# Sixty-four bytes: the place of eleven weight blocks in SBUF, in an attention and feed-forward kernel on one core

## The chip, the core and the metric

The kernel runs on one core of a Trainium2 chip. The metric is the device time of one execution in microseconds, taken as the median of several; before the change it is 888.88 us (three runs, 888.55 to 888.99). The profile shown here is one execution taken by the hardware profiler.

## The reference: what is computed

A pooled attention feeds a feed-forward layer. With 8 batches, 8 heads, 576 positions and head size 64:

```python
k_p = k.reshape(B, H, Sp, pool, D).mean(axis=3)      # pool = 8, Sp = 72
v_p = v.reshape(B, H, Sp, pool, D).mean(axis=3)
scores = scale * np.matmul(q, k_p.transpose(0, 1, 3, 2))
attn = softmax(scores)
x = matmul(attn, v_p), put together as (4608, 512)
h = x @ w_in                                          # w_in is 512 x 2048
g = np.maximum(h, 0.0) + np.log1p(np.exp(-np.abs(h))) # softplus
out = g @ w_out                                       # w_out is 2048 x 512
```

Everything is float32. Most of the arithmetic lies in the two products of the feed-forward layer.

## The kernel before

**Tiling.** The 4608 tokens are worked in 18 chunks of 256. The 2048 hidden columns are cut into 16 weight blocks of 128; block f has its part of w_in (512 x 128, stored as 128 x 512) and its part of w_out (128 x 512). To reach float32 accuracy each operand is split into a high and a low part of type fp32r, and each product is made of three: high by high, high by low, low by high.

**First product.** `ffn1_products` (L620) and `pair1` (L668) compute h. Here the weights (the stationary operand, which a LDWEIGHTS puts into the array) are 128 x 128 pieces of w_in out of the tiles `w` and `l`, and what streams past them (the moving operand) is x, 256 tokens wide.

**Second product.** Here it is the other way round: the stationary operand is a 128 x 128 piece of g (tiles `gh`, `gl` for the high and the low part, `so` for sums of quarters of g), and what streams is w_out. In the first four chunks (`ffn2`, L642; `pair2`, L709) a moving operand is 512 columns wide. From the fifth chunk on (`pair2_fast`, L817) the four quarter products of a pair of blocks are made from seven instead of eight products, each 256 columns wide. Three of the seven stream w_out itself; four stream sums of its quarters that `combine` made before, called t here. `t_sums`, `t_middle` and `streamed` say where these lie.

**Where the blocks lie.** Weight blocks 0 to 10 are in one SBUF tile, `w`, and blocks 11 to 15 in another, `l` (`LATE = 5`). In every partition such a tile holds n areas of 4096 bytes with w_out (high part, then low part; `parts(f)[:, 0]`), then a room of a few words, then n areas of 4096 bytes with w_in (`parts(f)[:, 1]`), then the room again. Once the first product has no more use for w_in in `w`, the t go over the same ground: `streamed(f)` is an area of 4096 bytes that is counted from the tile's start without the room.

**What sets addresses.** Tiles stand one behind the other in their pool, and `fill` puts a few unused words between them: `FILL[3]` words ahead of `w`, `FILL[0] - ROOM` behind it. Built, `w` begins at byte 10944 of each partition, which is 192 modulo 256. All 128 x 128 pieces of g that are loaded as weights of the second product (`gh`, `gl`, `so` and their like of the first chunks) begin at multiples of 256. The moving operand x of the first product lies at 192 modulo 256, the pieces of w_in that are its weights at 0, and w_out in `l` at 192. So before the change a streamed operand of either feed-forward product begins, modulo 256, 192 bytes after the weights that are loaded while it streams, which are those of the next matmul.

**Order of the work.** A list scheduler inside the kernel (`Order.run`, with a table of small corrections) fixes the order in which each engine gets its instructions; it knows nothing of addresses. SyncE issues all DMAs.

Of the kernel before, what the change touches and what calls it, by code (L numbers as in the profile page):

```python
# [10 lines left out]
F32R = mybir.dt.float32r  # L11
I32 = mybir.dt.int32
# [92 lines left out]
def pooled_attention_softplus_ffn(  # L105
# [12 lines left out]
    NTOK, DM = out.shape  # L118
    DFF = w_in.shape[1]
    P = 128  # L120
# [18 lines left out]
    wpool = ctx.enter_context(tc.tile_pool(name="wpool", bufs=1))  # L139
# [51 lines left out]

    PART, ROOM, LATE = 2 * DM, 16, 5
    BEGINS = [0, FC - LATE, FC]
    FILL = 256 - ROOM, 32, 16, 64
    groups = [None, None]

    def group(f):
        g = 0 if f < FC - LATE else 1  # L200
        n = BEGINS[g + 1] - BEGINS[g]
        if groups[g] is None:
            groups[g] = wpool.tile([P, 2 * (n * PART + ROOM)], F32R, tag="wl"[g], name="wl"[g])
        return groups[g], f - BEGINS[g], n

    def place(w, f, n):
# [2 lines left out]
    def parts(f):  # L209
        return place(*group(f)).rearrange("p i (a n) -> p i a n", a=2)  # L210

    def streamed(f):
        w, f, n = group(f)
        return w[:, (n + f) * PART:(n + f + 1) * PART]

    fill = lambda pool, n, i: n and pool.tile([P, n], F32, tag=f"fill{i}", name="fill")
    fill(wpool, FILL[3], 3)
    group(0)
    fill(wpool, FILL[0] - ROOM, 0)
    stage = wpool.tile([P, 2 * (LATE * PART + ROOM)], I32, tag="l", name="stage")  # L220
    stage_at = lambda i: stage[:, i * 2 * PART:(i + 1) * 2 * PART].rearrange("p (i n) -> p i n", i=2)
    fill(wpool, FILL[1], 1)
    for tag in ("Xha", "Xhb", "Xla", "Xlb"):
        xpool.tile([P, HP, CT], F32R, tag=tag, name="x")
    fill(xpool, FILL[2], 2)
    wi, wo = {}, {}
# [1328 lines left out]
```

## Time and profile before

| what | value |
|---|---|
| median of the runs | 888.88 us (888.55 to 888.99) |
| the profiled execution's own time | 888.88 us |
| its span, first to last instruction | 887.2 us |
| TensorE matmuls (PE), busy | 873.3 us, 98% of the span, 8280 instructions |
| weight loads (PEld), busy | 830.8 us, 94% |
| VectorE (DVE), busy | 646.4 us, 73% |
| ScalarE (ACT), busy | 416.6 us, 47% |
| granted TensorE clock, mean | 0.997 |

A matmul's duration in the profile is longer than its share of the engine's time, since the next begins while it still drains. How fast TensorE goes is therefore read from the distance between the starts of matmuls that follow each other, which the timeline gives: its rows merge neighbours of one kind, with the start of the first and their count.

### The profile page before, as it was taken

To read this page: it belongs to the slowest core of one execution; us is meant where nothing else is said; L and a number is where in the kernel's file an instruction comes from. 1 tells how busy PE (TensorE), PEld (TensorE's weight loads), DVE (VectorE), ACT (ScalarE), POOL (GpSimd) and SP (SyncE) were. 2 spreads that over 40 slices of the span, in tenths; PEclk is the share of its full clock that TensorE was granted. 3 is DMA by queue.
4 is the path that set the end of the run, shared out by engine and by line. 5 is a ranking of instruction groups with operands and counts; after the bars stand their busy time and mean duration, and the time that the engine had idled before them with its cause. 6 is when DMAs were issued, how large, how long until landed. Compare 5 with 4: busy or idle time off the path is not lost.

```text
span 887.2 us, 20509 instructions
## 1 busy us (share of the span) xinstructions
PE 873.3 (98%) x8280; PEld 830.8 (94%) x8280; DVE 646.4 (73%) x1601; ACT 416.6 (47%) x852; POOL 3.8 (0%) x33
## 2 busy tenths in 40 slices
PE   7999999999999999999999999999999999999997
PEld 4689998899999999999999999999999999999997
DVE  5899999788858788677776566778576565747454
ACT  5954343355353545445444435353545354535432
POOL 1000000000000000000000000000000000000000
PEclk9999999999999999999999999999999999999999
DMA  8966544445887778696877575678656565736472
GB/s 261 321 203 210 170 166 159 163 156 201 288 283 225 234 250 266 207 268 197 279 232 223 190 223 205 191 258 252 215 181 232 183 214 178 251 143 236 170 248 83
DMA packets 107086, 191.12 MB, mean 215 GB/s; under 512 B 46064, under 2 KB 60400, under 8 KB 106992
## 3 DMA queue, kind: packets, MB, share of 16 engines
q1 hardware_dynamic: 106992, 189.82, 65.3%
q8 instruction: 65, 1.06, 0.5%
q14 instruction: 29, 0.24, 0.1%
HBM read 167.25 MB, written 22.54 MB: 214 GB/s over the span
## 4 chain that ended last, share of the span: by engine, by line
PE 95%; DMA 2%; DVE 1%; ACT 1%; issue 0%; SPq 0%; DVEq 0%; ACTq 0%
PE h L668 37%; PE m L817 30%; PE acc L642 8%; PE h L620 7%; PE acc L709 3%; PE avp L587 2%; PE qTp L380 2%; PE ptp L461 2%; PE sc L508 1%; PE avp L594 1%; DMA l<-wi 1%; ACT E L425 1%; DMA kvl<-in_v_dram 1%; PE m L508 0%; PE sc L400 0%; PE ltp L561 0%
## 5 line engine op out<-in xcount | busy, mean ns | idle before, releaser
L668 PE MATMUL h<-x,l 128*128 128x256 f32 x2748 | 338.1, 279 | 1.0 <-DMA l<-wi 1.0
L668 PEld LDWEIGHTS h<-x,l 128*128 128x128 f32 x2748 | 324.0, 188 | 2.6 <-DMA l<-wi 1.4
L676 ACT ACTIVATE g<-h 128x512 f32<-128x512 f32 x120 | 71.8, 598 | 286.0 <-PE h L668 285.9
L817 PE MATMUL m<-w,so 128*128 128x256 f32 x1134 | 148.4, 278 | 0.0
L817 PEld LDWEIGHTS m<-w,so 128*128 128x128 f32 x1134 | 138.3, 188 | 0.1
L727 DVE TENSOR_TENSOR sf<-g 128x128 f32<-128x128 f32 x112 | 32.7, 292 | 136.5 <-ACT g L676 136.4
L741 ACT CAST so<-sf 128x512 fp32r<-128x512 f32 x112 | 69.7, 622 | 63.6 <-DVE sf L730 61.0
L817 PE MATMUL m<-w,gh 128*128 128x256 f32 x476 | 92.0, 282 | 0.0
L746 DVE TENSOR_TENSOR so<-sf,so 128x512 fp32r<-128x512 f32 x112 | 77.3, 690 | 17.9 <-ACT so L741 16.1
L817 PEld LDWEIGHTS m<-w,gh 128*128 128x128 f32 x476 | 72.1, 188 | 0.0
L697 DVE TENSOR_TENSOR gl<-g,gh 128x384 fp32r<-128x384 f32 (+1 forms) x120 | 67.2, 560 | 2.4 <-ACT gh L690 2.4
L817 PE MATMUL m<-w,gl 128*128 128x256 f32 x238 | 66.2, 278 | 0.0
L690 ACT ACTIVATE gh<-h 128x384 fp32r<-128x384 f32 (+1 forms) x120 | 59.3, 494 | 0.0
L625 ACT ACTIVATE g<-h 128x256 fp32r<-128x256 f32 x96 | 32.0, 382 | 55.5 <-PE h L620 33.5
L620 PEld LDWEIGHTS h<-x,w 128*128 128x128 f32 x396 | 48.6, 188 | 2.7 <-ACT g L625 0.6
L620 PE MATMUL h<-x,w 128*128 128x256 f32 x396 | 49.8, 278 | 0.2 <-ACT g L625 0.2
L817 PEld LDWEIGHTS m<-w,gl 128*128 128x128 f32 x238 | 44.9, 189 | 0.0
L838 DVE TENSOR_TENSOR o<-o,m 128x256 f32<-128x256 f32 x98 | 39.7, 418 | 4.0 <-PE m L817 0.9
L642 PE MATMUL acc<-w,g 128*128 128x512 f32 x132 | 41.9, 399 | 0.0
L817 PE MATMUL m<-l,gh 128*128 128x256 f32 x196 | 38.1, 283 | 0.0
L730 DVE TENSOR_TENSOR sf<-g,sf 128x128 f32<-128x128 f32 x112 | 32.7, 292 | 3.9
L431 DVE TENSOR_REDUCE sm<-E 128x8 f32<-128x576 f32 x30 | 21.2, 748 | 18.3 <-ACT E L343 18.3
(210 smaller groups left out, 1261.0 us busy)
## 6 DMA issues: line engine op xcount, KB each, us to landing
l<-wi SPq DMA_DIRECT2D x224, 512.0 KB
out_dram<-o SPq DMA_DIRECT2D x36, 256.0 KB
q<-in_q_dram SPq DMA_DIRECT2D x32, 256.0 KB
kst<-in_k_dram SPq DMA_DIRECT2D x24, 288.0 KB
vst<-in_v_dram SPq DMA_DIRECT2D x24, 256.0 KB
stage<-in_moe_w_in_dram SPq DMA_DIRECT2D x22, 256.0 KB
stage<-in_moe_w_out_dram SPq DMA_DIRECT2D x11, 512.0 KB
wi<-w SPq DMA_DIRECT2D x11, 512.0 KB
```

What stands on the lines that cost most here:

```text
L620: nc.tensor.matmul(out=ps[:, 0:CT], lhsT=row(w, kc), rhs=x[:, kc], start=first and kc == j == 0, stop=last and kc == KC - 1 and j == 2)
L642: nc.tensor.matmul(out=accs[c][t], lhsT=a[:, ts], rhs=w, start=f == 0 and j == 0, stop=f == FC - 1 and j == 2)
L668: nc.tensor.matmul(out=ps[:, k * CT:(k + 1) * CT], lhsT=row(w, kc), rhs=x_[c][i][:, kc], start=first and n == 0, stop=last and n == len(or ...
L676: nc.scalar.activation(out=g, in_=x.rearrange("p (b i) -> p b i", i=P), func=AF.Softplus)
L690: nc.scalar.activation(out=gh, in_=quarters(c, x.rearrange("p (b i) -> p b i", i=P)), func=AF.Softplus)
L697: nc.vector.tensor_tensor(out=gl, in0=quarters(c, g), in1=gh.bitcast(F32), op=ALU.subtract)
L727: tt(out=sf[:, 2], in0=g[:, 0], in1=g[:, 2], op=ALU.add)
L730: tt(out=sf[:, 3], in0=g[:, 3], in1=sf[:, 1], op=ALU.subtract)
L741: nc.scalar.copy(out=so[:, 0], in_=ss[c, u])
L746: nc.vector.tensor_tensor(out=so[:, 1], in0=sf, in1=so[:, 0].bitcast(F32), op=ALU.subtract)
L817: nc.tensor.matmul(out=ms[c][n], lhsT=x, rhs=y, start=u == 0 and j == 0 and n in (1, 6, 5, 4), stop=u == FP - 1 and j == 2 and n in (2, 7, ...
L838: nc.vector.tensor_tensor(out=o, in0=in0, in1=m[n], op=how)
```

## The change

The tile `w` gets a room of 32 words in place of 16, `l` keeps its 16; the filling ahead of `w` shrinks from 64 words to 48, and the filling behind it from 224 words to 208. In bytes of a partition: `w` begins 64 lower, at 10880 in place of 10944, and is 128 longer; everything behind it stands where it stood (16 words less ahead, 32 more inside, 16 less behind). The w_out areas of blocks 0 to 10 and the streamed t in `w` move 64 bytes down with the tile. The w_in areas in `w` do not move, since the room in front of them grew by what the start went down. So the streamed operands out of `w` begin at 128 modulo 256 in place of 192, against weights that begin at 0 as before. Every engine has the same instructions in the same order with the same waits.

```diff
-    PART, ROOM, LATE = 2 * DM, 16, 5
+    PART, ROOMS, LATE = 2 * DM, (32, 16), 5
     BEGINS = [0, FC - LATE, FC]
-    FILL = 256 - ROOM, 32, 16, 64
+    FILL = 208, 32, 16, 48
     groups = [None, None]

     def group(f):
         g = 0 if f < FC - LATE else 1
         n = BEGINS[g + 1] - BEGINS[g]
         if groups[g] is None:
-            groups[g] = wpool.tile([P, 2 * (n * PART + ROOM)], F32R, tag="wl"[g], name="wl"[g])
+            groups[g] = wpool.tile([P, 2 * (n * PART + ROOMS[g])], F32R, tag="wl"[g], name="wl"[g])
         return groups[g], f - BEGINS[g], n
...
     fill(wpool, FILL[3], 3)
     group(0)
-    fill(wpool, FILL[0] - ROOM, 0)
-    stage = wpool.tile([P, 2 * (LATE * PART + ROOM)], I32, tag="l", name="stage")
+    fill(wpool, FILL[0], 0)
+    stage = wpool.tile([P, 2 * (LATE * PART + ROOMS[1])], I32, tag="l", name="stage")
```

## The prediction

> **What bounds the kernel now.** First the page: busy times, the granted clock, and the chain of work that ended last.
>
> ```profile
> PE 873.3 (98%) x8280; PEld 830.8 (94%) x8280; DVE 646.4 (73%) x1601; ACT 416.6 (47%) x852; POOL 3.8 (0%) x33
> PEclk9999999999999999999999999999999999999999
> PE 95%; DMA 2%; DVE 1%; ACT 1%; issue 0%; SPq 0%; DVEq 0%; ACTq 0%
> PE h L668 37%; PE m L817 30%; PE acc L642 8%; PE h L620 7%; PE acc L709 3%; PE avp L587 2%; PE qTp L380 2%; PE ptp L461 2%; PE sc L508 1%; PE avp L594 1%; DMA l<-wi 1%; ACT E L425 1%; DMA kvl<-in_v_dram 1%; PE m L508 0%; PE sc L400 0%; PE ltp L561 0%
> ```
>
> TensorE is the end of 95% of the chain at full clock. No instruction moves, so the only way in which the change can reach the time is the distance from one matmul's start to the next. Second, the groups of TensorE instructions with their shapes kept apart: these are the matmuls whose moving operand comes out of `w`, and beside them the largest group, which streams x.
>
> ```profile
> line engine op names shapes xcount | busy us, mean ns | idle before us <-releasers
> L668 PE MATMUL h<-x,l 128*128 128x256 f32 x2748 | 338.1, 279 | 1.0 <-DMA l<-wi 1.0
> L817 PE MATMUL m<-w,so 128*128 128x256 f32 x1134 | 148.4, 278 | 0.0
> L817 PE MATMUL m<-w,gh 128*128 128x256 f32 x476 | 92.0, 282 | 0.0
> L817 PE MATMUL m<-w,gl 128*128 128x256 f32 x238 | 66.2, 278 | 0.0
> L642 PE MATMUL acc<-w,g 128*128 128x512 f32 x132 | 41.9, 399 | 0.0
> L642 PE MATMUL acc<-w,gl 128*128 128x512 f32 x66 | 26.2, 397 | 0.3 <-DVE gl L631 0.3
> L709 PE MATMUL acc<-w,gh 128*128 128x512 f32 x44 | 14.1, 402 | 0.0
> L709 PE MATMUL acc<-w,gl 128*128 128x512 f32 x22 | 8.7, 395 | 0.0
> ```
>
> So 1134 + 476 + 238 = 1848 matmuls of 256 columns and 132 + 66 + 44 + 22 = 264 of 512 columns are touched. Idle time before them is 0.3 us, so there is nothing to win from waits.
>
> Third, the timeline of TensorE at two places with the same kinds of instructions, us from the span's start, the row's length, and its count behind the x. The first is at 435 us:
>
> ```profile
> 435.68 1.58 PE L817 MATMUL m<-w,so 128*128 128x256 f32 x12
> 437.09 0.40 PE L817 MATMUL m<-w,gh 128*128 128x256 f32 x2
> 437.32 0.28 PE L817 MATMUL m<-w,gl 128*128 128x256 f32 x1
> 437.44 2.99 PE L668 MATMUL h<-x,l 128*128 128x256 f32 x24
> 440.27 0.40 PE L817 MATMUL m<-w,gh 128*128 128x256 f32 x2
> ```
>
> The second lies between 592 and 605 us:
>
> ```profile
> 592.57 1.52 PE L817 MATMUL m<-w,so 128*128 128x256 f32 x12
> 593.93 0.39 PE L817 MATMUL m<-w,gh 128*128 128x256 f32 x2
> ...
> 598.68 0.40 PE L817 MATMUL m<-w,gh 128*128 128x256 f32 x2
> 598.92 0.28 PE L817 MATMUL m<-w,gl 128*128 128x256 f32 x1
> ...
> 601.08 2.88 PE L668 MATMUL h<-x,l 128*128 128x256 f32 x24
> 603.80 1.04 PE L380 MATMUL qTp<-ident,q 128*128 128x128 f32 x8
> ```
>
> At 435 us, 12 matmuls that stream `w` take 437.09 - 435.68 = 1.41 us, 117.5 ns each, and 24 that stream x take 2.83 us, 117.9 ns each. At 592 us the 12 take 1.36 us, 113.3 ns each, and at 601 us the 24 take 2.72 us, 113.3 ns each. TensorE thus has **two cadences**, 4.5 ns apart, for the same instructions with the same addresses modulo 256, and both products share them. A cadence holds over long stretches, from one interruption by transposes or scores to the next. Other engines do not tell the two apart; busy times over most of such a stretch, the slow one first:
>
> ```profile
> 423.20:447.90 24.70, 24.70 (x212) 24.70 (x211) 20.70 (x60) 11.77 (x19) 0.00 (x0) 1.00 0.83 266
> 562.80:588.00 25.20, 25.20 (x225) 25.20 (x224) 19.32 (x56) 11.73 (x19) 0.00 (x0) 1.00 0.78 244
> ```
>
> In the columns PE, PEld, DVE, ACT and POOL busy, granted clock, DMA share and GB/s, 212 matmuls in 24.70 us stand against 225 in 25.20, at the same clock, with ACT alike and DVE at 84% against 77%. The slow cadence looks like a relation between the two reads of SBUF that TensorE makes at once, the moving operand and the next weights, that once begun repeats itself. By the distances of the starts in the trace, 579 of the 1848 touched matmuls go at the slow cadence (116 to 125 ns) and 1246 at the fast one (115 or less); among the untouched, 686 of the 2880 of L668 and 129 of the 503 of L817 that stream `l` are slow, and 2135 and 356 are fast.
>
> **The change part by part.** *What is removed or added:* no instruction, wait or transfer. The DMAs into `w` write the same bytes from the same sources 64 bytes lower, and VectorE and ScalarE write and read `w` there during conversion; they get no new work, and TensorE covers them (95% of the chain). Cost nothing; if they were slower, the 1.0 us that L668 waits for DMA in the group above shows how thin their share is.
>
> *What moves:* the moving operand begins 128 instead of 192 bytes after the next weights, modulo 256. No matmul before the change streams from `w` at 128, so the price has to be bounded. The nearest row at 128 is another instruction, a transpose (L380), whose moving operand, the identity, lies at byte 1152, that is 128 modulo 256. The weight loads (PEld) of such a group beside those of x:
>
> ```profile
> 600.97 2.79 PEld L668 LDWEIGHTS h<-x,l 128*128 128x128 f32 x24
> 603.71 0.89 PEld L380 LDWEIGHTS qTp<-ident,q 128*128 128x128 f32 x8
> 604.57 0.30 PEld L817 LDWEIGHTS m<-l,gh 128*128 128x128 f32 x2
> ```
>
> Eight loads in 0.86 us are 107.5 ns each, against 2.74 us / 24 = 114.2 for those beside x. That is faster, though the transposes stream half as many columns, and it says at least that a load beside a read at 128 is not held up. Lower end: all 1848 at 107.5, 1246 x 5.8 + 579 x 10.3 = 13.2 us gained. Upper end: all at the slow cadence, 1246 x 4.5 = 5.6 us lost. I take the value between them that a row of the same instruction has: all 1848 at 113.3, so that the 579 gain 4.5 ns each, **-2.6 us**. My reason is that the slow cadence is a pattern that holds on only while the offset stays the same from matmul to matmul, and now it changes with every turn from `w` to x.
>
> For the same reason some of the slow matmuls beside them gain. The 686 + 129 = 815 are worth 3.7 us if all become fast; those ahead of the first block of `w` in their stretch stay, those behind may change. Between nothing and 3.7 I take a third, **-1.2 us**.
>
> Each turn between streams at 128 and at 192 can cost a hiccup. Counted along L668 and L817 there are 280 turns. After an interruption two matmuls take 598.92 - 598.68 = 0.24 us, 120 ns each, 6.7 above the fast cadence. Between 0 and 280 x 6.7 = 1.9 us I take half, **+0.9 us**.
>
> The 264 wide ones:
>
> ```profile
> 202.48 0.62 PE L709 MATMUL acc<-w,gh 128*128 128x512 f32 x2
> ...
> 205.04 0.40 PE L709 MATMUL acc<-w,gl 128*128 128x512 f32 x1
> 205.28 0.96 PE L668 MATMUL h<-x,w 128*128 128x256 f32 x7
> ```
>
> From 202.48 to 205.28 us there are 12: 233.3 ns each, 6.7 more than twice 113.3. Between twice the fast and twice the slow cadence (235.6) that is -1.8 to +0.6 us; no row says which, and I take nothing.
>
> **Sum:** -2.6 - 1.2 + 0.9 = -2.9 us. The profiled execution took 888.88 us with a span of 887.2, and is itself the median, so I predict 886.0 us.
>
> **The rivals.**
>
> *Nothing changes.* The cadence is a matter of how a stretch begins, not of the offset: for it speaks that at the one offset 192 both cadences occur, and that 12 matmuls of `w` and 24 of x next to them agree to 0.4 ns. Against it speaks that the slow one repeats over two hundred matmuls, which something periodic in the addresses explains best. Some stretches begin anew and fall out otherwise, one of 210 matmuls being worth 0.9 us; the time stays at 888.9, give or take 1.5. The Trainium skill, "TensorE: Matmul & The Clock Gate", section "Part 2: What happens when you issue a matmul", speaks for this rival: TensorE has two independent read ports, and loading the next weights takes no read bandwidth from the running matmul. By that rule no offset matters and the sum would be 0; the 4.5 ns between the rows at 437 and 601 us are nothing it accounts for. That the change does not do what it says belongs here too, with little chance, as the tile does begin 64 bytes lower.
>
> *Slower: 128 is the slow relation.* If the moving read at 128 meets the weight load once more in each matmul, the 1246 of `w` that now go at 113.3 go at 117.8: +5.6 us, with the turns' +0.9 that is 895.4. This decides from the point where more than 650 of the 1246 turn slow (650 x 4.5 = 2.9, what the forecast gains). If the slow cadence is then carried into the blocks of x and `l` between them, up to (2135 + 356) x 4.5 = 11.2 us more, 906.6. For it speaks that the cadence is seen to be carried from `w` to x (437.09 to 440.27); against it the 107.5 ns of the loads beside the transposes.
>
> *Much faster.* The loads go beside `w` as they do beside the transposes: the lower end, -13.2 us, 875.7. Against it: 256 columns stream where a transpose has 128, so the moving read may set the cadence and not the load.
>
> **How the numbers follow.** Forecast 0.34, much faster 0.04, nothing 0.29, slower 0.33, of which about 0.08 is above 897. The measurement tells about 0.2%, 1.8 us, from no change, so faster has 0.38, same 0.29, slower 0.33. The forecast's own range is 882 to 887.1 (-2.6 - 3.7 - 0.6 to the smallest gain that can be told). The range reaches up past 895.4 to 897, and down to 881.5 between the forecast's end and the much faster case: left out are about 0.05 below and 0.08 above.
>
> **What would show it.** After the change, the rows of 12 matmuls `m<-w,so` everywhere 1.36 us apart from what follows, none 1.41, with a mean duration of 276 instead of 278 ns in their group: right. Rows of 24 of x at 2.83 us become fewer: the second term is right. The first matmul behind a turn at 118 or more: the third. Wrong would be rows of 12 at 1.41 us as often as now (the first rival), or rows of 12 at 1.41 us in place of 1.36 (the second); a row of 12 at 1.30 us would be the lower end.

## The result and the profile after

The change makes the kernel **slower**: 897.72 us (896.96 to 898.23, three runs) against 888.88, a ratio of 1.0099 with a 95% interval of 1.0076 to 1.0122, or 8.8 us. I had forecast 886.0; the time lies just above my range and on the side of the rival at 895.4.

The page of the changed kernel first, the parts that answer to those shown of before. The busy times, the clock and the chain:

```profile
span 896.0 us, 20509 instructions
PE 882.5 (98%) x8280; PEld 840.6 (94%) x8280; DVE 647.1 (72%) x1601; ACT 416.2 (46%) x852; POOL 3.8 (0%) x33
PEclk9999999999999999999999999999999999999999
PE 95%; DVE 2%; DMA 1%; SPq 1%; ACT 1%; issue 0%; DVEq 0%; ACTq 0%
```

TensorE is busy 9.2 us longer, at the same clock, and still is 95% of the chain; no wait has come in its place. The groups of its instructions, shapes apart:

```profile
L668 PE MATMUL h<-x,l 128*128 128x256 f32 x2748 | 338.1, 279 | 0.0
L817 PE MATMUL m<-w,so 128*128 128x256 f32 x1134 | 153.2, 282 | 0.0
L817 PE MATMUL m<-w,gh 128*128 128x256 f32 x476 | 93.7, 285 | 0.0
L817 PE MATMUL m<-w,gl 128*128 128x256 f32 x238 | 67.3, 283 | 0.0
L642 PE MATMUL acc<-w,g 128*128 128x512 f32 x132 | 41.9, 399 | 0.0
L817 PE MATMUL m<-l,so 128*128 128x256 f32 x210 | 31.2, 279 | 0.0
```

The three groups that stream `w` in 256 columns went from means of 278, 282 and 278 ns to 282, 285 and 283; the group that streams x stands where it stood (279), and so do the wide ones (399). The timeline, at the place that was at 435 us before and at a later one:

```profile
438.74 1.59 PE L817 MATMUL m<-w,so 128*128 128x256 f32 x12
440.17 0.40 PE L817 MATMUL m<-w,gh 128*128 128x256 f32 x2
440.40 0.28 PE L817 MATMUL m<-w,gl 128*128 128x256 f32 x1
440.52 2.89 PE L668 MATMUL h<-x,l 128*128 128x256 f32 x24
443.25 0.40 PE L817 MATMUL m<-w,gh 128*128 128x256 f32 x2
...
738.77 1.59 PE L817 MATMUL m<-w,so 128*128 128x256 f32 x12
740.20 0.40 PE L817 MATMUL m<-w,gh 128*128 128x256 f32 x2
```

Twelve matmuls that stream `w` take 440.17 - 438.74 = 1.43 us, 119.2 ns each, and 1.43 us again at 739 us. Before they took 1.36 us or 1.41. The 24 that stream x right behind them take 2.73 us, 113.8 ns each: x finds its quicker cadence again.

Where the 8.8 us are, by the distances from one matmul's start to the next, summed over each kind in both traces: the 1848 of L817 out of `w` went from 214.0 to 221.5 us, +7.5; L668 and L620 -0.9 (before, L668 held one wait of 1.0 us for a DMA); L817 out of `l` +0.4; all 512-wide ones -0.1 together; the rest +1.9, of which 1.5 lies in the first 43 us. There the two profiled executions differ in the granted clock. These are the rows of the stretch from 35.1 to 38.5 us (columns as in the prediction, the clock third from the right), before and after the change:

```profile
35.10:38.50 3.40, 3.40 (x41) 3.23 (x40) 2.89 (x7) 3.37 (x19) 0.00 (x0) 1.00 1.03 363
35.10:38.50 3.40, 3.29 (x21) 2.96 (x23) 3.40 (x7) 2.95 (x18) 0.00 (x0) 0.51 1.03 323
```

At about half the clock the changed kernel falls from 1.1 us behind to 2.4 us behind, and it is 1.5 us behind at 43 us. Before, the half clock was granted from 8.0 to 11.5 us, and the clock shows no other drop until the end. Whether the change moved this drop or the execution did by chance is not shown, since each kernel has one trace.

### The profile page after: what moved, and what is told of

Its sections match the earlier page's. It is cut to its first block, busy times and chain, and to the rows that moved or that the text cites. A ratio compares the mean times of both kernels' runs of the same rounds, so it can differ in the third digit from the quotient of the medians.

```text
span 896.0 us, 20509 instructions
## 1 busy us (share of the span) xinstructions
PE 882.5 (98%) x8280; PEld 840.6 (94%) x8280; DVE 647.1 (72%) x1601; ACT 416.2 (46%) x852; POOL 3.8 (0%) x33
## 4 chain that ended last, share of the span: by engine, by line
PE 95%; DVE 2%; DMA 1%; SPq 1%; ACT 1%; issue 0%; DVEq 0%; ACTq 0%
PE h L668 37%; PE m L817 31%; PE acc L642 7%; PE h L620 7%; PE acc L709 3%; PE avp L587 2%; PE ptp L461 2%; PE qTp L380 2%; PE sc L508 1%; PE avp L594 1%; DMA stage<-in_moe_w_out_dram 1%; DMA kvl<-in_v_dram 1%; PE m L508 0%; PE ltp L561 0%; DVE o L838 0%; SPq L894 0%
## 5 line engine op out<-in xcount | busy, mean ns | idle before, releaser
L668 PE MATMUL h<-x,l 128*128 128x256 f32 x2748 | 338.1, 279 | 0.0
L668 PEld LDWEIGHTS h<-x,l 128*128 128x128 f32 x2748 | 324.9, 188 | 1.2
L817 PE MATMUL m<-w,so 128*128 128x256 f32 x1134 | 153.2, 282 | 0.0
L817 PEld LDWEIGHTS m<-w,so 128*128 128x128 f32 x1134 | 142.5, 188 | 0.0
L741 ACT CAST so<-sf 128x512 fp32r<-128x512 f32 x112 | 69.6, 621 | 63.6 <-DVE sf L730 61.5
L817 PE MATMUL m<-w,gh 128*128 128x256 f32 x476 | 93.7, 285 | 0.0
L817 PEld LDWEIGHTS m<-w,gh 128*128 128x128 f32 x476 | 72.8, 188 | 0.0
L817 PE MATMUL m<-w,gl 128*128 128x256 f32 x238 | 67.3, 283 | 0.0
L690 ACT ACTIVATE gh<-h 128x384 fp32r<-128x384 f32 (+1 forms) x120 | 59.2, 493 | 0.0
L620 PEld LDWEIGHTS h<-x,w 128*128 128x128 f32 x396 | 48.6, 188 | 2.6 <-ACT g L625 0.5
L620 PE MATMUL h<-x,w 128*128 128x256 f32 x396 | 49.8, 278 | 0.1
L817 PEld LDWEIGHTS m<-w,gl 128*128 128x128 f32 x238 | 44.9, 189 | 0.0
L642 PE MATMUL acc<-w,g 128*128 128x512 f32 x132 | 41.9, 399 | 0.0
L817 PE MATMUL m<-l,gh 128*128 128x256 f32 x196 | 38.1, 283 | 0.0
```

The source lines that it names most:

```text
L620: nc.tensor.matmul(out=ps[:, 0:CT], lhsT=row(w, kc), rhs=x[:, kc], start=first and kc == j == 0, stop=last and kc == KC - 1 and j == 2)
L642: nc.tensor.matmul(out=accs[c][t], lhsT=a[:, ts], rhs=w, start=f == 0 and j == 0, stop=f == FC - 1 and j == 2)
L668: nc.tensor.matmul(out=ps[:, k * CT:(k + 1) * CT], lhsT=row(w, kc), rhs=x_[c][i][:, kc], start=first and n == 0, stop=last and n == len(or ...
L690: nc.scalar.activation(out=gh, in_=quarters(c, x.rearrange("p (b i) -> p b i", i=P)), func=AF.Softplus)
L741: nc.scalar.copy(out=so[:, 0], in_=ss[c, u])
L817: nc.tensor.matmul(out=ms[c][n], lhsT=x, rhs=y, start=u == 0 and j == 0 and n in (1, 6, 5, 4), stop=u == FP - 1 and j == 2 and n in (2, 7, ...
```

## The experiments

The theory after the result: **the distance between the start of the moving operand and the start of the next weights, modulo 256, sets the cadence** ("distance" below always means this). Its rivals: only 192 has its quicker cadence because x has it too, and any turn between unequal distances costs; or it is the place of the moving operand itself that counts; or it is the address and not its remainder. "Steady" means of starts below are taken over matmuls of 256 columns that are at least the fourth in a row of one distance and no interruption.

**Other distances for `w` alone.** Room and filling are changed as in the change, in four other amounts (the lines of these cuts are shortened to the values); the w_in areas and everything behind `w` stay.

```diff
-    PART, ROOM, LATE = 2 * DM, 16, 5          # distance 192
-    FILL = 256 - ROOM, 32, 16, 64             # behind w: FILL[0] - ROOM = 224
+    ROOMS = (48, 16); FILL = 192, 32, 16, 32  # distance 64
+    ROOMS = (64, 16); FILL = 176, 32, 16, 16  # distance 0
+    ROOMS = (24, 16); FILL = 216, 32, 16, 56  # distance 160
+    ROOMS = (8, 16);  FILL = 232, 32, 16, 72  # distance 224
```

> w begins 128 bytes lower than before the change: its streamed operands lie 64 bytes after the next weights modulo 256. Theory A (the distance sets how often the moving read and the weight load meet, and 128 meets once more than 192): the 1848 matmuls of 256 columns out of w stay near the 119.9 ns of the change (221.5 us / 1848) or get worse, 897 us or more. Theory B (any distance other than that of x disturbs the cadence at the turns, the distance itself is nothing): the same as the change, 897.7, with the extra time at the turns. Theory C (cost falls off with the distance from one bad place): between 889 and 898.

> w begins 192 bytes lower than before the change: streamed operands and next weights begin alike modulo 256. Theory A: the two reads begin in the same place, the worst case, more than 897.7 us. Theory B: 897.7. Theory C: about 889 to 898.

> w begins 32 bytes lower than before the change, half of the change's step: distance 160. Theory A, if the places are 64 bytes wide: as the one or the other neighbour, 889 or 898; if the cost grows evenly: 893. Theory B: 897.7, since any distance other than 192 is a turn.

> w begins 32 bytes higher than before the change: distance 224. Theory A with an even growth: below 889, down to 884 (the 579 matmuls at the slower cadence gain 4.5 ns each and what follows them too). Theory B: 897.7.

Measured: 898.74, 897.10, 906.38 and 914.79 us against 889.37, ratios 1.0105 [1.0080, 1.0130], 1.0095 [1.0067, 1.0124], 1.0190 [1.0158, 1.0221] and 1.0280 [1.0254, 1.0306]. The group of `m<-w,so` in the four, in this order:

```profile
L817 PE MATMUL m<-w,so 128*128 128x256 f32 x1134 | 151.6, 279 | 0.0
```

```profile
L817 PE MATMUL m<-w,so 128*128 128x256 f32 x1134 | 153.7, 282 | 0.0
```

```profile
L817 PE MATMUL m<-w,so 128*128 128x256 f32 x1134 | 151.9, 280 | 0.0
```

```profile
L817 PE MATMUL m<-w,so 128*128 128x256 f32 x1134 | 152.4, 281 | 0.0
```

Against 148.4 us before, all are longer by 3 to 5 us, the change (153.2) among them. The steady means are 117.7, 119.7, 117.6 and 118.3 ns; 192 had 114.6. So there is no bad place from which the cost falls off, nor an even growth; there are no neighbours: 160 and 224, on either side of 192, lose like the rest. Distance 0 has the longest cadence of the four but the lowest total, where I had expected the highest; x gains beside it (L668 334.1 us from start to start, before 336.4).

Distance 64 needs a second look. Two of its blocks of `w`, at 313 and 455 us, go at the quicker cadence from end to end; most others go as the second group of rows here:

```profile
313.52 1.52 PE L817 MATMUL m<-w,so 128*128 128x256 f32 x12
314.88 0.39 PE L817 MATMUL m<-w,gh 128*128 128x256 f32 x2
...
444.22 1.57 PE L817 MATMUL m<-w,so 128*128 128x256 f32 x12
445.63 0.40 PE L817 MATMUL m<-w,gh 128*128 128x256 f32 x2
```

That is 1.36 us, 113.3 ns each, against 1.41 us, 117.5 ns each: the two cadences of 192. Distance 64 thus allows both, as 192 does, and differs in how seldom the quicker one is taken (2% against 71% of the steady matmuls). In this kernel x stays at 192, so a block of `w` is entered from x by a turn, or behind an interruption, as these two are; whether 64 would keep the quicker cadence if all streams had it was not tested.

The totals at 160 and 224 hold more than the cadence. In both, writes into `w` wait for the store of a neighbouring w_in area. Waits between 43 and 93 us, at 160:

```profile
ACT w L950 <- DMA wi<-w: 5.5, 1, 5.5
DVE w L954 <- DMA wi<-w: 2.9, 1, 2.9
```

Before, no wait for that store stands among those of this stretch. The instructions around it carry other waits than before in these two builds (rooms of 24 and 8 words), and in no other here; why the program orders them so was not followed up. Their traces also show the clock at 0.50 in this part of the run, from 57.3 to 60.7 and 94.8 to 98.2 us at 160 and from 91.8 to 98.6 us at 224; before, it is at 1.00 there. At 224 the x of L668 suffers too: of its 2880, 17% are 115 ns or less apart, before 74%. Behind its blocks of `w`, which go at a longer cadence, x goes at the longer cadence too:

```profile
L668 PE MATMUL h<-x,l 128*128 128x256 f32 x2748 | 344.9, 281 | 0.0
```

**Distance or place.** As in the change `w` streams from 128, but `l` and all g lie 64 bytes lower too, so that their weights begin at 192 and the distance is 192 again.

```diff
+    ROOMS = (32, 32); FILL = 192, 16, 0, 48
-  ...[:, 48:48 + HP * CT]   # x of the third chunk, in the pool of g
+  ...[:, 64:64 + HP * CT]
```

> As the change, and in addition the tile l and all tiles of g are 64 bytes lower, so that the weights of the second product begin at 192 modulo 256 and what streams past them at 128: the distance is 192 again, the place of the moving operand is that of the change. If the distance counts: 889, the 256-wide matmuls out of w at 115.8 ns on average as before. If the place of the moving operand itself counts: as the change plus the 504 matmuls out of l, 897.7 + 504 x 4 ns = 899.7.

Measured: 899.87 us against 888.46, 1.0120 [1.0089, 1.0152]. By the time alone this looked like the place; the trace says otherwise. The groups:

```profile
L668 PE MATMUL h<-x,l 128*128 128x256 f32 x2748 | 344.1, 281 | 0.0
L817 PE MATMUL m<-w,so 128*128 128x256 f32 x1134 | 147.7, 277 | 0.0
```

and its timeline, `w` and then x:

```profile
599.02 1.52 PE L817 MATMUL m<-w,so 128*128 128x256 f32 x12
600.38 0.39 PE L817 MATMUL m<-w,gh 128*128 128x256 f32 x2
...
607.66 2.99 PE L668 MATMUL h<-x,l 128*128 128x256 f32 x24
610.49 1.03 PE L380 MATMUL qTp<-ident,q 128*128 128x128 f32 x8
```

The twelve out of `w` take 1.36 us, 113.3 ns each, though they stream from 128. All 1848 take 214.1 us, before 214.0. **It is the distance**, at least between 128 and 192. What was lost is elsewhere. 3.9 us are lost before the 404th matmul, in the first 43 us. And x, whose addresses and weights were not touched, goes at 2.83 us / 24 = 117.9 ns (23% at 115 ns or less, 5.0 us more in sum). In this kernel the last matmul ahead of such a block of x streams from 128 against weights at 0, a single step at a distance of 128. Of the 67 blocks of x right behind `w`, all 67 go at the longer cadence (mean from the fifth matmul on above 115.5 ns), before 16; behind an interruption it is 10 of 33, as before. But the step alone does not decide it: in the change the same step stands ahead of x, behind a whole row at 128, and there only 14 of the 67 are long. What decides which cadence is taken up is not shown.

**The same distance everywhere, all places 64 lower.** To take away those turns one number is changed:

```diff
-    FILL = 256 - ROOM, 32, 16, 64
+    FILL = 256 - ROOM, 32, 16, 48
```

> One number alone: the filling ahead of w is 48 words in place of 64, with nothing given back behind it, so that w, l, x and g all lie 64 bytes lower. Every moving operand of the feed-forward products begins at 128 modulo 256 and every weight of theirs at 192; the distance is 192 throughout, at the turns too. If the distance alone counts: no change, 887.5 to 890, the matmuls of L817 out of w at the two cadences 113.3 and 117.8 with a mean near 114.6. If the place of the moving operand counts as well: about 907 and more, as where x streams from 128, plus the 7.5 us of the change.

Measured: 892.66 us against 889.45, 1.0037 [1.0023, 1.0051]: not 907, but not nothing. The groups:

```profile
L668 PE MATMUL h<-x,l 128*128 128x256 f32 x2748 | 337.9, 279 | 0.0
L817 PE MATMUL m<-w,so 128*128 128x256 f32 x1134 | 148.4, 278 | 0.0
```

They are those of before to 0.2 us (338.1 and 148.4). The 3.2 us that its span is longer lie ahead: the 100th matmul starts 3.7 us later. About half of that falls into a stretch in which this kernel's clock is at half, from 16.8 to 23.6 us, here before and in this kernel:

```profile
16.80:23.60 6.80, 6.36 (x108) 4.95 (x107) 6.46 (x16) 6.66 (x26) 0.00 (x0) 1.00 1.13 332
16.80:23.60 6.80, 6.04 (x20) 3.67 (x19) 5.63 (x11) 4.50 (x23) 0.00 (x0) 0.50 1.17 310
```

The delay is 1.3 us at the 20th matmul and 1.9 at the 90th, which starts at 17.2 us, and 3.7 at the 100th. Why the first part is lost, and why the half clock comes later and lasts longer than before (8.0 to 11.5 us), was not tested. The runs of the kernel before spread from 887.62 to 892.57 here (23 runs), so such starts may differ from execution to execution, but the interval says that this build's are late on average. In the traces of all the changed kernels here the 404th matmul starts 1.0 to 3.9 us later than in that of before, so a part of each total is start and not cadence.

**x at 128.** `w` and `l` as before, x 64 bytes lower.

```diff
+    ROOMS = (16, 16); FILL = 224, 16, 32, 64
+  ...[:, 32:32 + HP * CT]   # x of the third chunk
```

> w and l as before the change; x, the moving operand of the first product, is 64 bytes lower, so that it streams at a distance of 128 to its weights. If the distance counts for every stream: the 3456 matmuls that stream x go from 116.7 (403.3 us / 3456) to about 120 ns, +11 to +14 us, 900 to 903. If it is something of w alone: 889. If it is the turns between unequal distances: the same number of turns as in the change, 897.7, and long runs of x at 113.3.

Measured: 907.15 us against 888.46, 1.0208 [1.0178, 1.0237].

```profile
L668 PE MATMUL h<-x,l 128*128 128x256 f32 x2748 | 349.4, 283 | 0.2 <-DMA l<-wi 0.2
L817 PE MATMUL m<-w,so 128*128 128x256 f32 x1134 | 149.0, 278 | 0.0
```

```profile
612.96 3.01 PE L668 MATMUL h<-x,l 128*128 128x256 f32 x24
615.81 1.04 PE L380 MATMUL qTp<-ident,q 128*128 128x128 f32 x8
```

x now takes 2.85 us / 24 = 118.8 ns, in runs of 24 with no turn in them; its steady mean is 118.7, that of `w` in the change. L668 and L620 lose 11.2 and 2.5 us, 13.7 of the forecast 11 to 14, but the time is 4 us above the forecast: L817 out of `w` loses 1.7 without being touched, and the start 2.7. For a distance of 128, turns as the cause are out.

**`l` at 128, alone.**

```diff
+    ROOMS = (16, 32); FILL = 208, 16, 16, 64
```

> w as before the change; only l is 64 bytes lower, so that 504 matmuls of 256 columns stream at a distance of 128. If the distance counts: +504 x 4 ns = 2.0 us, 890.9, and those matmuls at about 120 ns in place of 117.7. If turns count: they are fewer than in the change, +1 to +3 us.

Measured: 899.04 us against 888.46, 1.0114 [1.0086, 1.0142]. That is 10.6 us for 504 matmuls, five times the 2.0 expected. `l` itself behaves as forecast, 59.2 to 61.5 us with a steady mean of 118.4 ns. The rest is carried: L817 out of `w`, at its old distance, loses 2.4 us (41% at 115 ns or less, before 67%), L668 1.6, L620 0.8; and 2.0 us lie in the first 43 us.

```profile
590.81 1.58 PE L817 MATMUL m<-w,so 128*128 128x256 f32 x12
592.23 0.40 PE L817 MATMUL m<-w,gh 128*128 128x256 f32 x2
...
598.92 2.88 PE L668 MATMUL h<-x,l 128*128 128x256 f32 x24
```

The twelve of 592.23 - 590.81 = 1.42 us, 118.3 ns each, stream `w` at 192.

**The remainder or the address.** The change with `w` 256 bytes higher.

```diff
+    ROOMS = (32, 16); FILL = 144, 32, 16, 112
```

> The change with w 256 bytes higher: same distance modulo 256, other addresses. If modulo 256 is what counts: 897.7. If it is the address itself or a larger modulus: anything else, 889 at best.

Measured: 899.78 us against 888.46, 1.0122 [1.0094, 1.0149]. The 1848 take 221.5 us as in the change, with the same 16% at 115 ns or less; the 2 us above the change's time lie in the first 43 us (+3.6 there against +1.5). Of two places 256 bytes apart one is as bad as the other.

**Between the steps.** All areas inside `w` and `l` 16 bytes higher, without and with a shift of the tiles, so that w_out and x are at distances 16 bytes off the earlier ones.

```diff
     def place(w, f, n):
-        return w.rearrange("p (i n) -> p i n", i=2)[:, :, f * PART:(f + 1) * PART]
+        return w.rearrange("p (i n) -> p i n", i=2)[:, :, 4 + f * PART:4 + (f + 1) * PART]
...
-        return w[:, (n + f) * PART:(n + f + 1) * PART]
+        return w[:, 4 + (n + f) * PART:4 + (n + f + 1) * PART]
# the second kernel also:
-    FILL = 256 - ROOM, 32, 16, 64
+    FILL = 256 - ROOM, 24, 16, 56
```

> Inside w and l all areas lie 16 bytes higher: w_out streams at a distance of 208 (w and l), and x, whose weights lie in w and l, at 176. If the quicker cadence of 113.3 ns needs a distance of 192 exactly: none of the 256-wide matmuls of L668 and L817 has it, all near 118 to 119, 5807 matmuls by some 3 ns, about +18 us, 907. If it needs only the neighbourhood of 192 (16 bytes to either side): 889.

> The same step of 16 bytes the other way with all tiles behind w lower: w_out streams at a distance of 240, x at 144. Both lie 16 bytes from distances whose matmuls went at 118.3 to 119.7 (224 and 0, 128 and 160). If only 192 is quick: 905 to 912. If there is another quick place on the grid of 16 bytes, its group shows distances of 113 or less between starts and the time falls below 900.

Measured: 911.88 and 915.77 us against 889.92, 1.0244 [1.0227, 1.0262] and 1.0289 [1.0273, 1.0304]. In the first:

```profile
L668 PE MATMUL h<-x,l 128*128 128x256 f32 x2748 | 349.3, 282 | 0.0
L817 PE MATMUL m<-w,so 128*128 128x256 f32 x1134 | 152.6, 282 | 0.0
```

Both products lose. With these two the steady means, at all distances tried, are:

| distance | stream | steady mean, ns | 115 ns or less |
|---|---|---|---|
| 0 | w | 119.7 | 0% |
| 64 | w | 117.7 | 2% |
| 128 | w (the change) / x / l | 118.7 / 118.7 / 118.4 | 21 / 20 / 25% |
| 144 | x | 119.9 | 17% |
| 160 | w | 117.6 | 18% |
| 176 | x | 118.8 | 2% |
| 192 | w before / w streaming from 128 | 114.6 / 114.0 | 71 / 87% |
| 208 | w | 118.3 | 18% |
| 224 | w | 118.3 | 4% |
| 240 | w | 117.2 | 21% |

Only at 192 does the quicker cadence hold for most matmuls, and besides 192 only 64 has rows of it, the two blocks above. At the other eight distances no two matmuls in a row are each followed by the next start within 114 ns; what is 115 ns or less there is part of a pattern: at 128, starts follow each other by 115, 117, 122, 120 and 119 ns over and over.

**A version that might beat both.** In the kernel with `w` at 0 the 512-wide matmuls of L642 had a steady mean of 227.0 ns, at 192 they have 233.7. So only their weights are moved.

```diff
-        g = one.tile([P, CT], F32R if tag[:2] == "gh" else F32, tag=tag, name="g")
+        g = one.tile([P, 3 * P], F32R, tag=tag, name="g")[:, 48:48 + CT] if tag[:2] == "gh" else one.tile([P, CT], F32, tag=tag, name="g")
...
-        gl = one.tile([P, CT], F32R, tag="gl" + name, name="gl")
+        gl = one.tile([P, 3 * P], F32R, tag="gl" + name, name="gl")[:, 48:48 + CT]
```

> The kernel before, but the weights gh and gl of the 512-wide matmuls of the first three chunks begin 192 bytes further into their tiles, so that the distance of the 288 matmuls of L642 is 0 in place of 192; all others keep theirs. By the run in which w lay at 0, the wide ones take 227.0 ns in place of 233.6: 288 x 6.6 ns = 1.9 us less, 887.0. If the wide ones gain for another reason than the distance: 888.9. If the turn to a distance of 0 and back spoils the cadence of x between them (the 576 of L620 went from 66.9 to 68.3 us there): 888.5.

Measured: 890.50 us against 889.45, 1.0014 [1.0000, 1.0027]. It does not beat the kernel before. The wide ones gain only 0.8 us, with 229.0 ns out of `w`, since turns break their rows; and the x of L620 between them loses 1.6, since behind the wide ones at 0 it goes at the longer cadence. Of the 1.4 us by which its span is longer than that of before, 1.15 lie in the first 43 us. The longer cadence of x between the wide ones:

```profile
86.06 1.58 PE L620 MATMUL h<-x,w 128*128 128x256 f32 x12
87.47 0.63 PE L642 MATMUL acc<-w,g 128*128 128x512 f32 x2
```

1.41 us for twelve, 117.5 ns; the third of the expectations, with a larger price than it gave.

## Why the prediction was wrong

**The bound** held: no instruction moved, TensorE stayed 95% of the chain, and the time came through the distance between starts. The counts of 1848 and 264 were the right ones, and there were two cadences to reckon with.

**The step that failed** is the first term: "all 1848 at 113.3, so that the 579 gain 4.5 ns each, -2.6 us", with its reason that "the slow cadence is a pattern that holds on only while the offset stays the same". The runs showed the reverse. It is the 113.3 that is bound to the distance: it is common at 192, was taken by two blocks at 64, and at the other eight distances, 128 among them, there is no row of it, in runs of 24 without a turn either. In place of -2.6 the 1848 cost +7.5 us. I had read two cadences at one distance as a sign that the longer one was the special case, because it was the rarer.

**The bounds of that term** were too narrow above. I took the longer cadence seen before, 117.8, as the worst, +5.6 us. At 128 the matmuls have a cadence of their own, 118.7, which no row of before could show. The lower bound, from loads beside transposes at 107.5 ns, was not informative: there 128 columns stream, and the row was picked by the identity's place, 128, without the place of the weights beside it, so its distance was not known.

**Second term**, -1.2 for slow x and `l` that break out: nothing. L668 has 796 of its matmuls at 116 to 125 ns in place of 686 and its sum is the same but for the DMA wait; `l` loses 0.4. **Third term**, +0.9 for hiccups at 280 turns: not found. Steady 118.7 x 1848 is 219.4 us of 221.5, so 2.1 us lie outside the steady rows, before 214.0 - 1848 x 114.6 = 2.2. **The wide ones**, taken at nothing: right (-0.05 us), though their pattern changed, from 231 and 236 ns in turn to 229 and 238. **Not in the sum at all:** the start, 1.5 us later, with the half clock at 35 us.

**The rivals.** "128 is the slow relation" was what happened, by its own condition (more than 650 of the 1246): 16% of the 1848 are left at 115 ns or less. Its 895.4 falls short of 897.72 by the size of the cadence (1.9 us) and the start. That the longer cadence is then carried into x did not happen in the change, but does with `l` at 128, with `w` at 224, and where a single step at 128 stands ahead of x. "Nothing changes" is out: moving one of the two reads by 64 bytes costs 4.1 ns in each of these matmuls (118.7 against 114.6), and moving both together costs them nothing (214.1 us against 214.0). With it goes the sum of 0 that the prediction drew from the Trainium skill ("TensorE: Matmul & The Clock Gate", "Part 2: What happens when you issue a matmul"), by which loading the next weights takes no read bandwidth from the running matmul; the measurement decides. One thing that spoke for this rival holds all the same: at 192, and at 64, both cadences occur at one distance, so the distance alone does not fix the time. The chances stood at 0.33 for slower and 0.38 for faster. I had written that no matmul before the change streams from `w` at 128; with no row for the price, the range should have reached further than 897.

What is not shown is the mechanism: that the moving read and the weight load meet in SBUF fits the dependence on their distance modulo 256, but nothing in the records shows such a meeting.

## What to carry to other kernels

Where TensorE streams one matmul after the other with a weight load beside each, look at the distance from start to start, not at the busy share: here a few ns per matmul, by the place of one operand relative to the weights loaded beside it, are 1 to 3% of the time. Keep one distance for all streams that follow each other, measure it before choosing it, and move moving operand and weights together when a tile has to move. When the price of a place has no row in the profile, bound it by more than the worst row seen.

## What was not expected of the hardware

Of ten distances on a grid of 16 bytes (0, 64 and 128 to 240), one alone, 192, lets most 256-wide fp32r matmuls start 113.3 ns apart; 16 bytes to either side the means are 118.3 and 118.8, and 64 has two blocks at 113.3 and else 117.7. For 512-wide ones another distance is quicker: 227.0 ns at 0 against 233.7 at 192. And a cadence has memory: with 504 matmuls put at a worse distance, 2.4 us were lost in others that had kept theirs.
